# Two of six blocks of exponentials go through ScalarE and GpSimd instead of ScalarE and VectorE, in a kernel of attention and two expert layers

## The chip, the cores and the metric

The kernel runs on one core of one Trainium2 chip. The metric is device time in microseconds (us) from one launch; lower is better. The engines are TensorE (PE in the profile; its weight loads are listed apart as PEld), VectorE (DVE), ScalarE (ACT), GpSimd (POOL) and SyncE (SP), which issues the DMAs.

## The reference

Attention over 16 heads (2 batches of 8) of 768 positions and 64 dimensions, in which a query sees only the keys that fall to the same of 16 centroids, then two expert layers:

```python
mask = q_assign[:, :, :, None] == k_assign[:, :, None, :]
scores = scale * np.matmul(q, k.transpose(0, 1, 3, 2))
scores = np.where(mask, scores, -1000000000.0)
attn = np.exp(scores - np.max(scores, axis=-1, keepdims=True))
attn = attn / (np.sum(attn, axis=-1, keepdims=True) + 1e-09)
out = np.matmul(attn, v)
...
g = softplus(x @ w_in)            # 512 -> 2048
x = g @ w_out                     # 2048 -> 512
P = sinkhorn(exp(x @ w_gate))     # 8 rounds, 8 experts
out += P[:, e:e + 1] * (np.maximum(x @ w1[e], 0.0) @ w2[e])
```

## The kernel before

**Attention.** Two heads make a pair; there are eight pairs. The 768 queries of a head are cut in two, so that a pair is four halves, and the stage is a run of 32 halves, numbered `i`. For a half, `score` makes three tiles of scores (128 queries by 768 keys, four products each on TensorE, L478), VectorE takes each tile's maximum (L486), and ScalarE makes the exponentials `E` with their sum (L491).

`e_trans(i, s, ph)` then treats the keys in six blocks `s` of 128. Phase 0 turns a block of the half's three `E` tiles on TensorE into one PSUM tile `t` of 128 keys by 384 queries (L518, three transposes). The product with the values is to be more precise than one rounded product, so the block is split into a rounded part and a rest: phase 1 copies `t`, rounded, to `eh` in SBUF (ScalarE, L521), and phase 2 takes `el = t - eh` (VectorE, L525). `av(i, s)` adds the two products with the values, `eh` and `el`, to one PSUM tile `av` of the half (L533). `merge` takes that tile out (ScalarE L545, VectorE L547) and, at each second half, divides by the sums (VectorE L549).

**What a pair needs besides**, made ahead of time for a later pair: splitting queries and keys (`HL`; ScalarE L336, then GpSimd L344 and L345), splitting the values (`VV`; GpSimd L49 and L361), and finding each position's centroid (`sm`, `tp`, `po` on TensorE, copies by ScalarE, `A`, `mx` and `OH` on VectorE L402 to L410, with one product on GpSimd, L405, and one step, L413). `copy_r` at L49 is GpSimd's copy with rounding; `rw` spreads the sums, also there. Late in the stage GpSimd splits the four parts of the first layer's input (`chA`, `clA`; L49 and L99). Early in it the first weights, which come as 64-bit numbers, are converted to 32 bits by `to32` (L119 to L123, ScalarE and VectorE).

**What sets the order.** Every piece of work is put on a list with a time counted in steps; six steps are one half. The list is sorted by that time and traced in this order, and a scheduler then orders each engine's own queue by what is ready; the queues are fixed before the run, and each engine takes its queue in that order. A block's transposes stand at step `6 * i + s`, its products `AVL = 2` steps later.

**Buffers.** The PSUM tiles `t` (with `sm`, `tp`, `po`, `rb`) have three buffers, the score tiles two, `av` one; `eh` and `el` have four each, `E` seven.

The two expert layers follow (L631 and L684 the first products, L740 and L759 the second). Their code is not touched, and in the changed kernel each engine's queue holds the same instructions in the same order there.

Of the kernel before, what the change touches and what calls it, by code (L numbers as in the profile page):

```python
# [7 lines left out]
F32 = mybir.dt.float32  # L8
F32R = mybir.dt.float32r
# [3 lines left out]
ALU = mybir.AluOpType  # L13
# [7 lines left out]
def attention_moe_moe2(ctx, tc, v, qt, kt, centroids, w_in, w_out, w_gate, w1, w2, eye, out, dbg=None):  # L21
    nc = tc.nc
# [6 lines left out]
    P = 128  # L29
    NT = S // P  # L30
    HT = NT // 2
    CB = HT * P
# [15 lines left out]
    def copy_r(out_, in_):  # L48
        nc.gpsimd.tensor_scalar(out_, in_, 1.0, 0.0, ALU.mult, ALU.add)  # L49
# [193 lines left out]
    ap = slot_pool["ap"] = att.enter_context(tc.tile_pool(name="ap", bufs=2))  # L243
# [67 lines left out]
    def at(step, fn, cat=None):  # L311
        events.append((step, len(events), fn, cat))
# [147 lines left out]
            P_(g * SP - 21.67 + 2 * j, "v", pair_vsplit, j)  # L460

    EB = 7
    AH, FU = -5, -3
    Et, SC, RB, EHL, AVt, TT, TM, RW = {}, {}, {}, {}, {}, {}, {}, {}

    def half(i):
        g, r = divmod(i, 4)
        hf, j = divmod(r, 2)
        return pairs[g], j, hf

    def score(i, t, ph):
        st, j, hf = half(i)
        if ph == 0:
            c = (hf * HT + t) * P
            ps = Et[i, t] = ps_s.tile([P, 2, 512], F32, tag="s", name=f"s{i}_{t}")
            for m, X in enumerate((st.AT, st.Bt)):
                for kk in range(2):
                    nc.tensor.matmul(  # L478
                        ps[:, kk, 0:CB], X[0, j][:, c : c + P], X[1, j][:, kk * CB : (kk + 1) * CB],
                        start=m == 0, stop=m == 1,  # L480
                    )
            return
        if ph == 1:
            if t == 0:
                SC[i] = SC[i - 1] if j else ap.tile([P, 3, 2, HT], F32, tag="sc", name=f"sc{i}", bufs=3)
            nc.vector.tensor_reduce(SC[i][:, 0, j, t : t + 1], Et[i, t][:, :, 0:CB], AX.XY, ALU.max, negate=True)  # L486
            return
        sc = SC[i]
        if ph == 2:
            e = ap.tile([P, S], F32, tag="E", name=f"E{i}_{t}", bufs=EB)  # L490
            nc.scalar.activation(  # L491
                e.rearrange("p (a c) -> p a c", a=2), Et[i, t][:, :, 0:CB], AF.Exp,
                bias=sc[:, 0, j, t : t + 1], scale=1.0, accum_out=sc[:, 1, j, t : t + 1],
            )
            Et[i, t] = e
            return
        if ph == 3:

            nc.vector.tensor_scalar(sc[:, 2], sc[:, 1], 1e-9, None, ALU.add)
            nc.vector.reciprocal(sc[:, 2], sc[:, 2])  # L500
            return
        if ph == 4:
            rw = ap.tile([P, HT, P], F32, tag="rw", name=f"rw{i}", bufs=1)
            copy_r(
                rw.rearrange("p t (j d) -> p t j d", j=2),
                sc[:, 2].rearrange("p j t -> p t j").unsqueeze(3).to_broadcast([P, HT, 2, D]),
            )
            RW[i] = rw
            return
        rb = RB[i] = ps_t.tile([P, CB], F32, tag="t", name=f"rb{i}")  # L510
        for t_ in range(HT):
            nc.tensor.transpose(rb[:, t_ * P : (t_ + 1) * P], RW[i][:, t_, :], idf)

    def e_trans(i, s, ph):
        if ph == 0:
            pt = TT[i, s] = ps_t.tile([P, CB], F32, tag="t", name=f"t{i}_{s}")
            for t in range(HT):
                nc.tensor.transpose(pt[:, t * P : (t + 1) * P], Et[i, t][:, s * P : (s + 1) * P], idf)  # L518
        elif ph == 1:
            eh = ap.tile([P, CB], F32R, tag="eh", name=f"eh{i}_{s}", bufs=4)  # L520
            nc.scalar.copy(eh, TT[i, s])  # L521
            EHL[i, s] = eh
        else:
            el = ap.tile([P, CB], F32R, tag="el", name=f"el{i}_{s}", bufs=4)
            nc.vector.tensor_tensor(el, TT.pop((i, s)), EHL[i, s].bitcast(F32), ALU.subtract)  # L525
            EHL[i, s] = EHL[i, s], el

    def av(i, s):
        st, j, hf = half(i)
        if s == 0:  # L530
            AVt[i] = ps_a.tile([P, CB], F32, tag="a", name=f"av{i}")
        for n, m in enumerate(EHL.pop((i, s))):
            nc.tensor.matmul(  # L533
                AVt[i], st.VV[j][:, s, :], m, start=s == 0 and n == 0, stop=s == NT - 1 and n == 1
            )

    def merge(i, ph):
        st, j, hf = half(i)
        lo, hi = (slice(0, D), slice(D, P))
        main, other = (lo, hi) if j == 0 else (hi, lo)  # L540
        if j == 0 and ph == 0:
            TM[i] = TM[i + 1] = ap.tile([P, CB], F32, tag="tmp", name=f"tmp{i}", bufs=2)
        tmp = TM[i]
        if ph == 0:
            nc.scalar.copy(tmp[main], AVt[i][other])  # L545
        elif ph == 1:
            nc.vector.tensor_tensor(tmp[main], AVt.pop(i)[main], tmp[main], ALU.add)  # L547
        else:
            nc.vector.tensor_tensor(xt[st.b][:, st.hp, hf * CB : (hf + 1) * CB], tmp, RB.pop(i), ALU.mult)  # L549
# [6 lines left out]
    AVL = 2  # L556
# [3 lines left out]
    for i in range(NHALF):  # L560
        g = i // 4
        for t in range(HT):
            n = 6 * i + 2 * t - LEAD
            for ph, d in enumerate((0.28, 0.47, 2.31)):
                at(n + d, lambda i=i, t=t, ph=ph: score(i, t, ph), (f"s{ph}", g))
        if i % 2:
            at(n + 2.42, lambda i=i: score(i, 0, 3), ("s3", g))
            at(6 * i + 3.9, lambda i=i: score(i, 0, 4), ("rw", g))
            at(6 * i + 5 + AVL + 0.04, lambda i=i: score(i, 0, 5), ("rb", g))
        for s in range(NT):  # L570
            n = 6 * i + s
            for ph in range(3):
                at(n, lambda i=i, s=s, ph=ph: e_trans(i, s, ph), (f"e{ph}", g))
            at(n + AVL + 0.05, lambda i=i, s=s: av(i, s), ("av", g))
        for ph, d in enumerate((0.06, 1.22, 1.99)[: 2 + i % 2]):
            at(6 * i + 5 + AVL + d, lambda i=i, ph=ph: merge(i, ph), (f"m{ph}", g))
    at(14, lambda: fetch_first(0), ("fr", 0))
# [284 lines left out]
    for n, u in enumerate(units):  # L862
# [59 lines left out]
        if hold and held == NHOLD - 1:  # L922
            run(queue)
            for lu, q, cols in late:
                if (0, lu[2]) not in PB:
                    load_p(0, lu[2])
                g = GF[lu, q][:, cols]
# [41 lines left out]
```

## Time and profile before

| | |
|---|---|
| median of three runs | 1612.45 us (1611.81 to 1612.92) |
| the profiled execution | 1614.17 us, its span 1612.3 us |
| granted clock of TensorE, mean | 0.995 |
| PE busy over the span | 1539.4 us (95%) |
| PEld | 1383.9 us (86%) |
| DVE | 1060.6 us (66%) |
| ACT | 837.2 us (52%) |
| POOL | 640.2 us (40%) |

The shares are means over two different stages: attention up to 285.42 us, where the last `av` tile is taken out, and the expert layers after it. Over the whole span PE is busiest; that says little about the first stage, which is the one that the change touches. Matmuls are pipelined and their ends are modelled, so the time from one weight load to the next is the better measure of what TensorE needs.

### The profile page before, as it was taken

To read this page: it belongs to the slowest core of one execution; us is meant where nothing else is said; L and a number is where in the kernel's file an instruction comes from. 1 tells how busy PE (TensorE), PEld (TensorE's weight loads), DVE (VectorE), ACT (ScalarE), POOL (GpSimd) and SP (SyncE) were. 2 spreads that over 40 slices of the span, in tenths; PEclk is the share of its full clock that TensorE was granted. 3 is DMA by queue.
4 is the path that set the end of the run, shared out by engine and by line. 5 is a ranking of instruction groups with operands and counts; after the bars stand their busy time and mean duration, and the time that the engine had idled before them with its cause. 6 is when DMAs were issued, how large, how long until landed. Compare 5 with 4: busy or idle time off the path is not lost.

```text
span 1612.3 us, 22512 instructions
## 1 busy us (share of the span) xinstructions
PE 1539.4 (95%) x8110; PEld 1383.9 (86%) x8110; DVE 1060.6 (66%) x1723; ACT 837.2 (52%) x1685; POOL 640.2 (40%) x611
## 2 busy tenths in 40 slices
PE   5899999989999999999999999989999999999998
PEld 4788888878897878899999999978999999999997
DVE  4899999998454768665555655577555556556563
ACT  4888888766576754343443434344434434343342
POOL 2323322334655743433334433345333343333440
PEclk9999999999999999999999999999999999999999
DMA  8556420464211211322223222223223222222211
GB/s 222 156 152 153 128 65 6 141 219 133 77 53 53 65 53 55 84 59 82 82 60 88 64 77 79 72 66 115 67 75 89 57 85 71 71 88 63 79 53 47
DMA packets 132545, 141.24 MB, mean 88 GB/s; under 512 B 9072, under 2 KB 96592, under 8 KB 132432
## 3 DMA queue, kind: packets, MB, share of 16 engines
q1 hardware_dynamic: 132288, 139.72, 30.5%
q8 instruction: 64, 1.05, 0.3%
q14 instruction: 49, 0.40, 0.1%
q10 hardware_dynamic: 144, 0.07, 0.0%
HBM read 107.72 MB, written 11.58 MB: 74 GB/s over the span
## 4 chain that ended last, share of the span: by engine, by line
PE 65%; DVE 7%; ACT 4%; issue 1%; POOL 1%; DMA 1%; DVEq 0%; SPq 0%; ACTq 0%; POOLq 0%
PE Y L759 32%; PE la L631 16%; PE mb L631 8%; PE lb L631 4%; PE y L740 2%; DVE gf L707 1%; DVE gl L721 1%; DVE wl L226 1%; ACT gh L720 1%; ACT u L705 1%; PE p L684 1%; ACT u L704 1%; DMA r<-in_moe_w_out_dram 1%; DVE xS L75 0%; ACT u L706 0%
## 5 line engine op out<-in xcount | busy, mean ns | idle before, releaser
L720 ACT CAST gh<-gf 128x384 fp32r<-128x384 f32 x316 | 161.3, 513 | 479.0 <-DVE gf L714 434.5
L214 POOL TENSOR_TENSOR wf<-wf 128x256 f32<-128x256 f32 x288 | 235.0, 837 | 344.9 <-DMA wf<-in_moe_w_dram 289.6
L232 POOL TENSOR_TENSOR w2l<-w2f,w2h 128x512 fp32r<-128x512 f32 x160 | 236.3, 1496 | 323.2 <-ACT w2h L231 323.2
L759 PE MATMUL Y<-w2h,gh 128*128 128x512 f32 x768 | 299.3, 390 | 0.6 <-ACT gh L720 0.6
L759 PE MATMUL Y<-w2l,gh 128*128 128x512 f32 x768 | 299.2, 390 | 0.0
L759 PE MATMUL Y<-w2h,gl 128*128 128x512 f32 x768 | 298.8, 390 | 0.0
L721 DVE TENSOR_TENSOR gl<-gf,gh 128x384 fp32r<-128x384 f32 x316 | 201.1, 640 | 95.9 <-ACT gh L720 89.3
L658 DVE TENSOR_TENSOR gf<-la,c 128x384 f32<-128x384 f32 x71 | 39.5, 557 | 254.5 <-PE la L631 254.2
L225 ACT CAST wh<-wf 128x512 fp32r<-128x512 f32 (+1 forms) x232 | 153.0, 684 | 39.0 <-PE la L631 28.8
L759 PEld LDWEIGHTS Y<-w2h,gl 128*128 128x128 f32 x768 | 144.2, 188 | 29.8
L759 PEld LDWEIGHTS Y<-w2h,gh 128*128 128x128 f32 x768 | 144.1, 188 | 22.2 <-ACT gh L720 1.1
L759 PEld LDWEIGHTS Y<-w2l,gh 128*128 128x128 f32 x768 | 144.3, 188 | 21.0
L226 DVE TENSOR_TENSOR wl<-wf,wh 128x512 fp32r<-128x512 f32 (+1 forms) x194 | 151.4, 806 | 0.9 <-ACT wh L225 0.9
L714 DVE SCALAR_TENSOR_TENSOR gf<-gf,pb 128x384 f32<-128x384 f32 x177 | 149.3, 844 | 4.0
L525 DVE TENSOR_TENSOR el<-t,eh 128x384 fp32r<-128x384 f32 x192 | 102.4, 549 | 10.0 <-ACT eh L521 8.7
L486 DVE TENSOR_REDUCE sc<-s 128x1 f32<-128x768 f32 x96 | 91.1, 950 | 20.7 <-PE s L478 20.6
L521 ACT CAST eh<-t 128x384 fp32r<-128x384 f32 x192 | 91.4, 480 | 21.9 <-PE t L518 13.1
L518 PE MATMUL t<-idf,E 128*128 128x128 f32 x576 | 98.1, 278 | 4.8 <-ACT OHT L426 2.8
L631 PE MATMUL mb<-chS,wh 128*128 128x384 f32 x288 | 98.4, 342 | 4.3 <-DVE gf L654 4.0
L231 ACT CAST w2h<-w2f 128x512 fp32r<-128x512 f32 x160 | 92.2, 617 | 16.9 <-PE y L740 8.7
L631 PE MATMUL la<-chA,wh 128*128 128x384 f32 x288 | 98.0, 340 | 1.9 <-DVE gf L714 1.9
L631 PE MATMUL la<-chS,wh 128*128 128x384 f32 x288 | 97.9, 340 | 0.2 <-ACT c L650 0.2
(181 smaller groups left out, 3381.9 us busy)
## 6 DMA issues: line engine op xcount, KB each, us to landing
w2f<-in_moe_w_dram SPq DMA_DIRECT2D x128, 256.0 KB, 3.2
wf<-in_moe_w_dram SPq DMA_DIRECT2D x128, 256.0 KB, 3.3
AT<-HL SPq DMA_DIRECT2D x64, 192.0 KB, 4.0
r<-in_moe_w_in_dram SPq DMA_DIRECT2D x16, 512.0 KB, 5.7
r<-in_moe_w_out_dram SPq DMA_DIRECT2D x16, 512.0 KB, 4.9
Bt<-HL SPq DMA_DIRECT2D x32, 192.0 KB, 4.0
pb<-pdram SPq DMA_DIRECT2D x15, 384.0 KB, 7.3
w<-wf SPq DMA_DIRECT2D x16, 256.0 KB, 3.4
```

The source lines that it names most:

```text
L214: nc.gpsimd.tensor_tensor(wf[:, SLOT[o_], :], wf[:, SLOT[u_], :], wf[:, SLOT[v_], :], ALU.subtract)
L225: nc.scalar.copy(wh[:, c0:c1], wf[:, c0 + o : c1 + o, :])
L226: (nc.vector if kind == 2 or u == (1, 0, 0, 0) else nc.gpsimd).tensor_tensor(wl[:, c0:c1], wf[:, c0 + o : c1 + o, :], wh[:, c0:c1].bitcast ...
L231: nc.scalar.copy(w2h[:, c], w2f[c])
L232: nc.gpsimd.tensor_tensor(w2l[:, c], w2f[c], w2h[:, c].bitcast(F32), ALU.subtract)
L518: nc.tensor.transpose(pt[:, t * P : (t + 1) * P], Et[i, t][:, s * P : (s + 1) * P], idf)
L525: nc.vector.tensor_tensor(el, TT.pop((i, s)), EHL[i, s].bitcast(F32), ALU.subtract)
L631: nc.tensor.matmul(ps, wt[:, s_, ks], xx[:, k_, :], start=i in (0, 1, 3) and n == 0, stop=n == 3 * nk - 1, skip_group_check=True,)
L714: nc.vector.scalar_tensor_tensor(g, src, 0.0, PB[sb, e][:, cols], ALU.max, ALU.mult)
L720: nc.scalar.copy(gh[:, cols], g)
L721: nc.vector.tensor_tensor(gl[:, cols], g, gh[:, cols].bitcast(F32), ALU.subtract)
L759: nc.tensor.matmul(y[m], gt[:, ms], wt[:, q, :], start=first and i == 0, stop=last and i == 2)
```

## The change

Of the six blocks of a half, those with `s` 0 and 3 take another way. ScalarE copies the PSUM tile unrounded to a new SBUF tile `tf` (two buffers); GpSimd makes the rounded part `ph` from it (`copy_r`) and the rest `pl = tf - ph` (two buffers each). The products of these two blocks come at step `+ 2.03` instead of `+ 0.05`, that is about two steps later. As block 0 is then no longer the first to be multiplied, block 1 opens the sum in PSUM.

```diff
+    BY_POOL, AV_FIRST = (0, 3), 1
...
+        elif s in BY_POOL:
+            if ph == 1:
+                pt, tf = TT[i, s], ap.tile([P, CB], F32, tag="tf", name=f"tf{i}_{s}", bufs=2)
+                nc.scalar.copy(tf, pt)
+                TT[i, s] = tf
+                return
+            tf = TT.pop((i, s))
+            eh = ap.tile([P, CB], F32R, tag="ph", name=f"ph{i}_{s}", bufs=2)
+            el = ap.tile([P, CB], F32R, tag="pl", name=f"pl{i}_{s}", bufs=2)
+            copy_r(eh, tf)
+            nc.gpsimd.tensor_tensor(el, tf, eh.bitcast(F32), ALU.subtract)
+            EHL[i, s] = eh, el
...
-        if s == 0:
+        if s == AV_FIRST:
             AVt[i] = ps_a.tile([P, CB], F32, tag="a", name=f"av{i}")
...
-                AVt[i], st.VV[j][:, s, :], m, start=s == 0 and n == 0, stop=s == NT - 1 and n == 1
+                AVt[i], st.VV[j][:, s, :], m, start=s == AV_FIRST and n == 0, stop=s == NT - 1 and n == 1
...
-            at(n + AVL + 0.05, lambda i=i, s=s: av(i, s), ("av", g))
+            at(n + AVL + (2.03 if s in BY_POOL else 0.05), lambda i=i, s=s: av(i, s), ("av", g))
```

On TensorE, in half 16 (pair 4), the queue before held the products in the order of the blocks. These rows begin behind the transposes of block 4 (`t16_4`); `s18_0` is a score tile of half 18.

```order
L533 MATMUL av16_2230<-eh16_2_2226,VV40_1753 128x384
L533 MATMUL av16_2230<-el16_2_2228,VV40_1753 128x384
L478 MATMUL s18_0_2274<-AT410_1593,AT400_1547 128x384 x2
L478 MATMUL s18_0_2274<-Bt410_1594,Bt400_1548 128x384 x2
L518 MATMUL t16_5_2288<-idf_65,E16_0_2049 128x128
L518 MATMUL t16_5_2288<-idf_65,E16_1_2105 128x128
L518 MATMUL t16_5_2288<-idf_65,E16_2_2155 128x128
L533 MATMUL av16_2230<-eh16_3_2252,VV40_1753 128x384
L533 MATMUL av16_2230<-el16_3_2254,VV40_1753 128x384
```

The same place of the changed kernel, again behind the transposes of block 4; `ph16_0` and `pl16_0` are the parts of block 0 that GpSimd made.

```order
L546 MATMUL av16_2321<-ph16_0_2249,VV40_1800 128x384
L546 MATMUL av16_2321<-pl16_0_2250,VV40_1800 128x384
L546 MATMUL av16_2321<-eh16_2_2292,VV40_1800 128x384
L546 MATMUL av16_2321<-el16_2_2294,VV40_1800 128x384
L479 MATMUL s18_0_2342<-Bt410_1638,Bt400_1592 128x384
L519 MATMUL t16_5_2356<-idf_65,E16_0_2109 128x128
L519 MATMUL t16_5_2356<-idf_65,E16_1_2164 128x128
L519 MATMUL t16_5_2356<-idf_65,E16_2_2219 128x128
```

Block 0 is now multiplied after block 1 and just ahead of block 2, and block 3 (not in these rows) after block 4, ahead of block 5. From a block's transposes to its products TensorE now passes some three further blocks of transposes, one score tile and about two blocks' products.

On GpSimd, in the same half, the queue before held only what a later pair needs and the `rw` tiles.

```order
L49 TENSOR_SCALAR VV51_2281<-rawv5_1661 128x6x64
L361 TENSOR_TENSOR VV51_2281<-rawv5_1661,VV51_2281 128x6x64
L345 TENSOR_TENSOR HL16_2301<-rT16_2133,HL16_2301 128x768
L405 TENSOR_TENSOR A5_2038<-A5_2038,wsel_89 128x384
L413 TENSOR_SCALAR OH5_2299<-OH5_2299 128x6x32
```

The changed kernel has the new copies and differences between them.

```order
L49 TENSOR_SCALAR ph16_0_2249<-tf16_0_2247 128x384
L530 TENSOR_TENSOR pl16_0_2250<-tf16_0_2247,ph16_0_2249 128x384
L49 TENSOR_SCALAR VV51_2349<-rawv5_1707 128x6x64
L361 TENSOR_TENSOR VV51_2349<-rawv5_1707,VV51_2349 128x6x64
L405 TENSOR_TENSOR A5_2098<-A5_2098,wsel_89 128x384
L345 TENSOR_TENSOR HL16_2367<-rT16_2195,HL16_2367 128x768
L49 TENSOR_SCALAR ph16_3_2317<-tf16_3_2315 128x384
L530 TENSOR_TENSOR pl16_3_2318<-tf16_3_2315,ph16_3_2317 128x384
L49 TENSOR_SCALAR ph17_0_2375<-tf17_0_2373 128x384
L530 TENSOR_TENSOR pl17_0_2376<-tf17_0_2373,ph17_0_2375 128x384
L413 TENSOR_SCALAR OH5_2365<-OH5_2365 128x6x32
```

`ph16_3` now waits in the queue behind the two `VV` instructions, `A5` and `HL16` of the next pair, and `OH5` behind the parts of the next half's block 0. In halves 26 and 27 the four `chA` and four `clA` instructions stand in the same way between `ph` and `pl` instructions.

On VectorE, the conversion of the first weights is placed otherwise. In the changed kernel these rows stand between `x0` of half 3 and `el4_4`, the rest of block 4 of half 4 (`cm`, `wf0` and `w2f` are the conversion; `sc` the maxima of score tiles).

```order
L122 SCALAR_TENSOR_TENSOR wf0_590<-r10_584,wf0_590 128x512
L487 TENSOR_REDUCE sc6_898<-s6_2_959 128x1
L487 TENSOR_REDUCE sc6_898<-s7_0_1008 128x1
L123 SCALAR_TENSOR_TENSOR wf0_590<-r10_584,wf0_590 128x512
L120 TENSOR_SCALAR cm001_2180<-cm001_2180 128x512
L487 TENSOR_REDUCE sc6_898<-s7_1_1036 128x1
L121 TENSOR_SCALAR wf0_590<-cm001_2180 128x512
L487 TENSOR_REDUCE sc6_898<-s7_2_1070 128x1
L122 SCALAR_TENSOR_TENSOR wf0_590<-r10_584,wf0_590 128x512
L120 TENSOR_SCALAR cm010_2222<-cm010_2222 128x512
L123 SCALAR_TENSOR_TENSOR wf0_590<-r10_584,wf0_590 128x512
```

They are the core of a run of 21 instructions (six maxima, eleven of the conversion) without a block's rest between them. Before, the conversion was spread from half 4 to half 15, and behind `x0` of half 3 the rests of blocks 3 to 5 of half 4 came after five other instructions.

## Rows read from the trace of the kernel before

**Rows 1.** Busy time of each engine in the two stages, attention first.
```profile
core 0: us, PE busy (x) PEld busy (x) DVE busy (x) ACT busy (x) POOL busy (x), PEclk, DMA share, GB/s
0.00:285.42 285.42, 249.95 (x1554) 223.89 (x1554) 242.76 (x451) 222.08 (x489) 86.36 (x113) 0.99 0.47 125
285.42:1612.30 1326.88, 1289.46 (x6556) 1159.97 (x6556) 817.79 (x1272) 615.12 (x1197) 553.89 (x498) 1.00 0.27 80
```

**Rows 2.** Same view: four stretches of four halves each, 126.07 to 252.35; the next stretch.
```profile
sum 126.28, PE 118.41 PEld 107.63 DVE 118.38 ACT 107.86 POOL 43.06; mean PE 29.60 PEld 26.91 DVE 29.60 ACT 26.96 POOL 10.77
...
252.35:280.54 28.19, 26.37 (x173) 24.01 (x173) 25.70 (x47) 23.42 (x53) 4.62 (x4) 1.00 0.00 1
```

**Rows 3.** Groups of VectorE, 126.07 to 252.35: count, busy us, mean ns, idle before.
```profile
L525 DVE TENSOR_TENSOR el<-t,eh 128x384 fp32r<-128x384 f32 x97 | 51.9, 548 | 2.8 <-ACT eh L521 2.2
L486 DVE TENSOR_REDUCE sc<-s 128x1 f32<-128x768 f32 x48 | 45.6, 950 | 3.2 <-PE s L478 3.2
```

**Rows 4.** Waits of weight loads, 126.07 to 252.35: us, times, longest.
```profile
PEld av L533 <- DVE el L525: 3.2, 4, 0.9
PEld t L518 <- ACT OHT L426: 2.9, 4, 0.7
```

**Rows 5.** Timeline of weight loads in half 20: start us, us, instruction.
```profile
203.08 0.19 PEld L533 LDWEIGHTS av<-eh,VV 128*128 128x128 f32 x1
203.36 0.42 PEld L518 LDWEIGHTS t<-idf,E 128*128 128x128 f32 x3
203.76 0.19 PEld L533 LDWEIGHTS av<-eh,VV 128*128 128x128 f32 x1
...
204.75 0.36 PEld L478 LDWEIGHTS s<-AT,AT 128*128 128x128 f32 x2
205.44 0.42 PEld L518 LDWEIGHTS t<-idf,E 128*128 128x128 f32 x3
206.68 0.19 PEld L533 LDWEIGHTS av<-el,VV 128*128 128x128 f32 x1 [0.65 <-DVE el L525]
```

**Rows 6.** Groups of ScalarE, 126.07 to 252.35.
```profile
L521 ACT CAST eh<-t 128x384 fp32r<-128x384 f32 x96 | 45.9, 481 | 8.0 <-PE t L518 5.3 <-PE av L533 0.5
L376 ACT COPY sT<-sm 128x384 f32<-128x384 f32 x8 | 3.8, 471 | 0.0
```

**Rows 7.** Groups of GpSimd, 126.07 to 252.35.
```profile
L345 POOL TENSOR_TENSOR HL<-rT,HL 128x768 fp32r<-128x768 f32 x6 | 11.3, 1890 | 3.1 <-ACT HL L336 2.8
L361 POOL TENSOR_TENSOR VV<-rawv,VV 128x384 fp32r<-128x384 f32 x8 | 8.1, 1010 | 0.7
L49 POOL TENSOR_SCALAR VV<-rawv 128x384 fp32r<-128x384 f32 x8 | 4.1, 512 | 19.8 <-PE av L533 19.8
...
L405 POOL TENSOR_TENSOR A<-A,wsel 128x384 f32<-128x384 f32 x4 | 4.0, 1006 | 5.5 <-DVE sc L499 5.0 <-DVE A L403 0.5
L99 POOL TENSOR_TENSOR clA<-x,chA 128x768 fp32r<-128x768 f32 x2 | 3.6, 1844 | 0.0
L49 POOL TENSOR_SCALAR chA<-x 128x768 fp32r<-128x768 f32 x4 | 3.3, 837 | 0.0
```

**Rows 8.** Two VectorE lines: ns min/median/max, first and last start.
```profile
L525 DVE TENSOR_TENSOR el<-t,eh x192: 507/550/560, 34.2 to 284.3; 128x384 fp32r<-128x384 f32 x192
...
L403 DVE TENSOR_TENSOR A<-A,mx x8: 547/621/1033, 14.9 to 236.2; 128x384 f32<-128x384 f32 x8
```

**Rows 9.** Timeline around the longest L403, GpSimd and VectorE.
```profile
171.48 1.84 POOL L345 TENSOR_TENSOR HL<-rT,HL 128x768 fp32r<-128x768 f32 x1 [1.40 <-ACT HL L336]
...
172.70 1.03 DVE L403 TENSOR_TENSOR A<-A,mx 128x384 f32<-128x384 f32 x1
```

**Rows 10.** Busy time of each engine in halves 4 and 5 (columns of rows 1).
```profile
67.78:80.73 12.95, 9.84 (x59) 8.12 (x58) 12.65 (x25) 9.59 (x20) 6.58 (x8) 0.96 0.59 151
80.73:89.51 8.78, 8.12 (x43) 7.15 (x44) 6.71 (x14) 6.21 (x14) 1.13 (x1) 0.67 0.37 91
```

## The prediction

> **What bounds the kernel now.** I read the two stages first, since the change touches one alone. Attention takes 285.42 of 1612.30 us; the expert layers keep every queue as it was, so their 1326.88 us stay as a block and move with the end of attention [rows 1]. The whole effect has to come out of the 285 us, in which VectorE is busy for 242.76 and TensorE loads weights for 223.89.
>
> Next I cut the steady part of attention into stretches of four halves, one pair's worth. Four of them take 126.28 us, 31.57 each. In 31.57 us VectorE is busy for 29.60, ScalarE for 26.96, GpSimd for 10.77 [rows 2]. VectorE is idle for only 1.97 us of a stretch (6%). TensorE has to be measured by pitch. A block, three transposes and its two products, takes 203.08 to 203.76, 0.68 us; the transposes alone 203.36 to 203.76, 0.40, so 0.13 each and 0.28 for the products; a score tile 204.75 to 205.44, 0.69 [rows 5]. A stretch has 24 blocks (16.3), 12 score tiles (8.3), 8 products for the centroids at a quarter of a score tile (1.4) and 18 more transposes (2.4): 28.4 us. TensorE could thus do a stretch in 28.4 and takes 31.57, because VectorE is the slowest hand: the longest waits of its weight loads are for `el` (3.2 us in four stretches; in half 20 it stood 0.65 us for one) and for a copy behind a crowded ScalarE (2.9) [rows 4, 5]. In the last stretch, with nothing to prepare, VectorE's load falls to 25.70 and the time to 28.19 [rows 2]: the time follows VectorE's load.
>
> **The change part by part.**
>
> *Removed from VectorE:* 8 of 24 `el` in a stretch at 0.548 us, 4.4 us [rows 3]. VectorE falls from 29.60 to 25.2.
>
> *ScalarE:* each rounded copy becomes a plain one. The nearest rows are 0.481 us rounded and 0.471 unrounded, both out of PSUM [rows 6]; between -0.01 and 0 us each, taken as 0. ScalarE stays at 27.0. The PSUM tile of these blocks is free after one copy, no longer after copy and `el`.
>
> *Added to GpSimd:* per block a `copy_r` (0.512) and a difference (1.010), the same shape as the split of the values [rows 7]: 1.52 us, 12.2 for 8 blocks. GpSimd rises from 10.8 to 23.0 us of a stretch of about 30. It has the time, but not at every moment (below).
>
> *TensorE:* the same products, so 28.4 stays. After the change it needs most, then ScalarE 27.0, VectorE 25.2, GpSimd 23.0. For a stretch the bounds are 28.4 (no wait at all, -3.2) and 31.57 (another wait takes the place of `el`, 0). I take TensorE's need plus the idle time that the busiest engine had before: 28.4 + 1.97 = 30.4, a gain of 1.2. For halves 6 to 27, that is 5.5 stretches, -6.6 us (bounds 0 and -17.6).
>
> *Last four halves:* weight loads are 24.01 there against 26.91 [rows 2], so TensorE's need is about 28.4 - 2.9 = 25.5; with 1.97 idle 27.5 instead of 28.19: -0.7 (bounds 0 and -2.7).
>
> *The wait that is added:* TensorE waits for `pl`, behind ScalarE and GpSimd. From the end of a block's transposes to its products its queue holds some four blocks' transposes, five pairs of products and a score tile or more, about 4.1 us at full pace. The new way is 0.48 + 0.51 + 1.01 = 2.0 us. So 2 us are left, if GpSimd is free. Behind a late `pl` stand all of TensorE's queue, and on GpSimd `OH` and `rw`, for which `po` and `rb` wait. `tf` has two buffers: a GpSimd that is two blocks late stops ScalarE, and with it the exponentials.
>
> *Where GpSimd is tight:* in half 16 `VV`, `A5` and `HL16` stand ahead of `ph16_3`. From the last product of half 15, which frees the buffer for `VV`, GpSimd needs 0.51 + 1.01 + 1.01 + 1.89 + 0.51 + 1.01 = 5.9 us [rows 7]; TensorE's queue up to the products of block 3 holds 5.6 us at full pace and 6.0 at the pace of 30.4. That is just in time: I count 0, and 1.9 (one `HL`) as the upper bound each time.
>
> *The input splits in halves 26 and 27:* four `chA` at 0.84 and four `clA` at 1.84 [rows 7] stand among three `ph`/`pl` pairs: 3.3 + 7.4 + 4.6 = 15.3 us of GpSimd where TensorE passes in 3 x 3.8 = 11.4. Of the 3.9 us the 2 in hand go off: TensorE stands for about 2 us. +2 (0 to +4).
>
> *The conversion in half 4:* half 4 took 12.95 us, and VectorE was busy for 12.65 of it; in half 5 the granted clock was 0.67, a mix of the levels 1.2 and 2.4 GHz, after a half in which TensorE was busy for only 9.84 of 12.95 [rows 10]. The run of 21 instructions now does much the same: six maxima at 0.95 and fifteen at the 0.51 of that half (12.65 / 25) are 13.3 us, against some 6 us of TensorE's queue. So half 4 stays as bad as it was. But half 5 then finds its scores made and VectorE nearly free; it took 8.78, and without three score tiles needs 7.1 - 2.1 = 5.0. I take -2: the bounds are -3.8 and +2.9, which is a second stay of 5.8 us at the lower level (0.33 of 8.78 us is lost). Halves 0 to 3: 0.
>
> *Does GpSimd slow VectorE?* `el` took 507 to 560 ns over all 192 [rows 8], with GpSimd busy or not: nothing is added there. But L403, which reads SBUF twice, took between 0.547 and 1.033 us, and the longest began while an `HL` was running (171.48 to 173.32) and ended 0.41 after it [rows 8, 9]. One L403 a stretch is +0.5 at most, on a VectorE with 5 us to spare: 0. [...]
>
> *Sum:* -6.6 - 0.7 + 2 - 2 = -7.3. The profiled execution was 1614.17 us, 1.9 more than its span and 1.7 above the median of the runs, 1612.45. 1614.17 - 7.3 = 1606.9, less 1.7: **1605 us**.
>
> **The rivals.**
>
> *TensorE gets all it asks for.* Nothing but its own need is left: -17.6 - 2.7 - 2, about -22, 1590; I give this case what lies below 1599. For it: all three other engines have at least 1.4 us less to do per stretch. Against it: in no stretch now does the busiest engine run without idle time, and ScalarE's 27.0 is close behind. 0.12.
>
> *ScalarE takes VectorE's place, so that nothing is gained.* The change doesn't relieve it: 27.0 us are in its queue in a fixed order, it copies, exponentiates and splits, and every block passes through it. Now it is idle for 4.6 us of a stretch, mostly for `t` and the maxima; if the chain transposes, copy, exponential, scores has its own length near 31 us, `el` was only its visible end. Then the stretch stays within 0.6 of 31.57, and the time within 3.2 us of 1612.45. Against it: the waits for `el` come first, and `OHT` is late behind work that partly waits for VectorE itself [rows 4, 6]. 0.22.
>
> *GpSimd is late and the kernel gets slower.* Place: `pl` behind an `HL`, `VV` or `A` of the next pair. If TensorE waits for one `HL` (1.89) per stretch, the stretch is 30.4 + 1.9 = 32.3, +0.7; over 5.5 stretches +3.9, and with the -0.7 for the last halves, +4 for the input splits and -2, about +5: 1618. With two per stretch it is 34.2 and about +16: 1628. It decides from 1.2 us of waiting for `pl` per stretch on. For it: the margin in half 16 is nil, and `A` and `HL` wait for VectorE and ScalarE in their turn. Against it: the load is 23 of 30 us, and at most places 2 us are in hand. The Trainium skill speaks for it ("GPSIMD Engine Reference", "Engine selection"): elementwise work belongs on VectorE, since GpSimd takes about twice as long for two inputs. The trace agrees on the ratio (1.010 against 0.548); by that rule the 8 differences cost 3.7 us more than they save, which is a loss only where GpSimd is waited for. 0.16.
>
> **How the numbers follow.** Forecast (1599 to 1609.2) 0.50, full gain 0.12, no change (1609.2 to 1615.7) 0.22, slower 0.16. A measurement of this kernel tells about 0.2%, 3.2 us, from no change. Faster: 0.50 + 0.12 = 0.62; same 0.22; slower 0.16. The range 1596 to 1616 leaves out the larger part of the slower case (about 0.13) and half of the full gain (0.06).
>
> **What would show it.** Right: the expert layers' 1326.9 us unchanged; attention ending near 278; stretches near 30.4 with VectorE busy for some 25 to 26, GpSimd for 23, TensorE's weight loads for 26.9 as now; waits for `el` nearly gone; `tf` copies at 0.47 to 0.48; one wait for `pl` of about 2 us in halves 26 and 27. Wrong: waits of TensorE or ScalarE for `pl` in every pair (GpSimd late), stretches of 31.5 with ScalarE's waits for TensorE grown (no gain), `el` longer than 0.56 while GpSimd works (contention), or a longer stay at 1.2 GHz around half 4 or in the input splits.

## The result and the profile after

The changed kernel takes 1627.69 us (median of four runs, 1626.45 to 1628.77) against 1612.13 for the kernel before, run beside it: a ratio of 1.0086, 95% interval 1.0073 to 1.0099. It is slower by 0.9%, and outside the range that was given.

The two stages of the profiled execution (columns as in [rows 1]):

```profile
0.00:299.38 299.38, 255.78 (x1554) 224.20 (x1554) 221.47 (x387) 221.94 (x489) 184.33 (x241) 0.94 0.46 119
299.38:1627.00 1327.62, 1289.90 (x6556) 1159.77 (x6556) 821.11 (x1272) 615.06 (x1197) 554.49 (x498) 1.00 0.27 80
```

The expert layers stayed as they were (1327.62 against 1326.88). Attention ends 13.96 us later, although VectorE is busy for 21.3 us less in it. The start of each half's merge (the first ScalarE copy of its `av` tile) cuts the stage into pieces that can be laid beside each other. Up to half 3's merge, where half 4 is counted from, the new kernel is 1.46 us later; half 4 takes 22.02 instead of 12.95 (+9.07); half 5 8.11 instead of 8.78 (-0.67); halves 6 to 25 157.83 instead of 157.53 (+0.30); from there to the end of attention 42.18 instead of 38.38 (+3.80). That is all of the 13.96. In the last piece halves 26 and 27, where the input splits are, take 17.63 instead of 13.64 (+3.99), and the rest 0.19 less.

The steady stretches, four of them (halves 10 to 25) from merge to merge, answer to [rows 2], which is 126.28 us long:

```profile
131.28:257.20 125.92, 119.30 (x777) 106.94 (x777) 102.71 (x176) 107.19 (x238) 84.07 (x106) 1.00 0.41 99
```

VectorE is busy for 25.7 us of a stretch of 31.48, GpSimd for 21.0, ScalarE for 26.8: the loads are as forecast, the length is not. What TensorE's weight loads now wait for in it (beside [rows 4]):

```profile
PEld av L546 <- DVE tmp L560: 5.2, 11, 1.0
PEld po L420 <- POOL OH L413: 4.0, 4, 1.7
PEld t L519 <- ACT E L492: 1.8, 8, 0.4
...
PEld av L546 <- POOL pl L530: 0.6, 2, 0.3
PEld av L546 <- DVE el L538: 0.5, 1, 0.5
```

Two rows of the same view of the kernel before, halves 10 to 25:

```profile
PEld po L420 <- POOL OH L413: 2.7, 4, 0.7
PEld av L533 <- DVE tmp L547: 1.2, 3, 0.8
```

The wait for `el` has nearly gone, as it should, and that for `OHT` (ScalarE's copy of `po`) too; longer waits for the merge (`tmp`) and for `OH` stand in their place. With all rows of the view added up, TensorE's weight loads waited for 14.5 us in these four stretches before and wait for 15.6 now. `pl` is hardly waited for.

Halves 4 and 5 (beside [rows 10]), and TensorE's waits in half 4:

```profile
69.24:91.26 22.02, 13.73 (x60) 10.43 (x59) 19.24 (x31) 12.17 (x25) 10.98 (x11) 0.72 0.49 130
91.26:99.37 8.11, 7.61 (x45) 6.62 (x44) 5.68 (x10) 5.87 (x13) 4.92 (x7) 0.71 0.61 168
```

```profile
PEld t L519 <- ACT tf L523: 3.9, 2, 3.1
PEld s L479 <- ACT E L492: 3.6, 3, 1.9
PEld av L546 <- DVE el L538: 2.1, 1, 2.1
PEld av L546 <- POOL pl L530: 1.3, 1, 1.3
```

VectorE in half 4, the first instruction of the run of 21 and the `el` behind it, then the weight load that waits for this `el` (all between left out):

```profile
72.14 0.55 DVE L402 TENSOR_REDUCE mx<-A 128x24 f32<-128x384 f32 x1
87.13 1.01 DVE L538 TENSOR_TENSOR el<-t,eh 128x384 fp32r<-128x384 f32 x2
```

```profile
87.73 0.29 PEld L546 LDWEIGHTS av<-el,VV 128*128 128x128 f32 x1 [2.08 <-DVE el L538]
```

And GpSimd in halves 26 and 27, with the three weight loads that wait for it (all loads between them, and GpSimd's rows after the third `clA`, left out):

```profile
263.50 0.52 POOL L49 TENSOR_SCALAR ph<-tf 128x384 fp32r<-128x384 f32 x1
263.97 1.83 POOL L99 TENSOR_TENSOR clA<-x,chA 128x768 fp32r<-128x768 f32 x1
265.75 1.01 POOL L530 TENSOR_TENSOR pl<-tf,ph 128x384 fp32r<-128x384 f32 x1
266.71 1.84 POOL L99 TENSOR_TENSOR clA<-x,chA 128x768 fp32r<-128x768 f32 x1
268.51 0.83 POOL L49 TENSOR_SCALAR chA<-x 128x768 fp32r<-128x768 f32 x1
269.43 1.82 POOL L99 TENSOR_TENSOR clA<-x,chA 128x768 fp32r<-128x768 f32 x1
271.22 0.51 POOL L49 TENSOR_SCALAR ph<-tf 128x384 fp32r<-128x384 f32 x1
```

```profile
266.82 0.19 PEld L546 LDWEIGHTS av<-pl,VV 128*128 128x128 f32 x1 [1.63 <-POOL pl L530]
...
271.78 0.19 PEld L546 LDWEIGHTS av<-ph,VV 128*128 128x128 f32 x1 [1.67 <-POOL ph L49]
272.85 0.19 PEld L546 LDWEIGHTS av<-pl,VV 128*128 128x128 f32 x1 [0.89 <-POOL pl L530]
```

A `clA` of 1.83 us lies between a `ph` and its `pl`, and three instructions of 4.5 us ahead of the next `ph`.

### The profile page after: what moved, and what is told of

Read it like the earlier page. It is cut to its first block, busy times and chain, and to the rows that moved or that the text cites. A ratio compares the mean times of both kernels' runs of the same rounds, so it can differ in the third digit from the quotient of the medians.

```text
span 1627.0 us, 22559 instructions
## 1 busy us (share of the span) xinstructions
PE 1545.7 (95%) x8110; PEld 1384.0 (85%) x8110; DVE 1042.6 (64%) x1659; ACT 837.0 (51%) x1685; POOL 738.8 (45%) x739
## 3 DMA queue, kind: packets, MB, share of 16 engines
q1 hardware_dynamic: 132288, 139.72, 30.4%
## 4 chain that ended last, share of the span: by engine, by line
PE 65%; DVE 7%; ACT 4%; issue 1%; POOL 1%; DVEq 0%; ACTq 0%
PE Y L772 32%; PE la L644 16%; PE mb L644 9%; PE lb L644 4%; PE y L753 3%; DVE gf L720 1%; DVE gl L734 1%; PE p L697 1%; DVE wl L226 1%; ACT u L718 1%; ACT gh L733 1%; ACT u L717 1%; DVE xS L75 1%; ACT wh L225 1%; ACT u L719 1%
## 5 line engine op out<-in xcount | busy, mean ns | idle before, releaser
L727 DVE SCALAR_TENSOR_TENSOR gf<-gf,pb 128x384 f32<-128x384 f32 x177 | 154.8, 876 | 4.0
L644 PE MATMUL la<-clS,wh 128*128 128x384 f32 x288 | 97.7, 339 | 0.0
L644 PE MATMUL mb<-clS,wh 128*128 128x384 f32 x288 | 97.7, 339 | 0.0
```

The source lines that it names most:

```text
L644: nc.tensor.matmul(ps, wt[:, s_, ks], xx[:, k_, :], start=i in (0, 1, 3) and n == 0, stop=n == 3 * nk - 1, skip_group_check=True,)
L727: nc.vector.scalar_tensor_tensor(g, src, 0.0, PB[sb, e][:, cols], ALU.max, ALU.mult)
```

## The experiments

Theory A, formed from these two traces: the loss sits in two places, half 4 and the input splits; in the steady stretches other waits took the place of `el`. Rival B: GpSimd is late or in the way everywhere, and VectorE's relief by itself would have gained. The runs came in four sets, each beside runs of the kernel before on the same chip; its medians there were 1614.71 (e1 to e4), 1614.34 (e5 to e8), 1613.53 (e9 to e12) and 1613.73 (e13 to e15). Lengths of halves are from merge to merge.

### Where the loss sits

**e1**, the change from half 8 on:

```diff
-    BY_POOL, AV_FIRST = (0, 3), 1
+    def by_pool(i, s):
+        return s in (0, 3) and i >= 8
```

> Halves 0 to 7 are treated as before the change, halves 8 to 31 as after it. Theory A (the loss sits in two places, the run of conversions in half 4 and the input splits in halves 26 and 27, and the steady stretches are unchanged because other waits took the place of those for el): half 4 falls from 22 us back to about 13, the time from 1627.7 to about 1619. Theory B (GpSimd's added work costs a little everywhere, by late pl and by contention): a quarter of the halves is relieved, so a quarter of the 15 us goes, about 1624.

1619.74 us, 1.0037 (1.0025 to 1.0050). Half 4 is 12.95 us, the last halves stay long (half 27's interval 11.67).

**e2**, in halves 8 to 25 alone:

```diff
+        return s in (0, 3) and 8 <= i < 26
```

> Only halves 8 to 25 go through GpSimd, so both half 4 and halves 26 and 27 are as before the change. Theory A: both losses are gone and the steady stretches bring nothing, 1611 to 1615. Theory B: 18 of 32 halves still pay, about 1620. If the relief of VectorE gained in the steady stretches what the prediction said (1.2 us each), it would be 1607.

1616.52 us, 1.0007 (0.9994 to 1.0021): no difference that can be told, though the time itself lies above A's range. Both places are as before (half 4 12.96, half 27 7.07). Eighteen halves of the new way, with VectorE busy for 10 us less over attention (232.60), gain nothing. A has the places right; the little that it hoped to gain (down to 1611) isn't there.

**e3**, VectorE's relief without GpSimd's work. It leaves out the remainder of blocks 0 and 3 of the kernel before (the rounded part is multiplied twice):

```diff
+            if s in (0, 3):
+                TT.pop((i, s))
+                EHL[i, s] = EHL[i, s], EHL[i, s]
+                return
             el = ap.tile([P, CB], F32R, tag="el", name=f"el{i}_{s}", bufs=4)
```

> The kernel before, without the difference el in blocks 0 and 3 (the rounded part is multiplied twice in its place, so that part of the computation is left out): VectorE is relieved by the same 64 instructions, ScalarE keeps its copies, and GpSimd gets nothing. Theory A: stretches stay near 31.4 us, since TensorE then waits for the merge of the av tile and for po; half 4 is still long, about 20 us, because its queue on VectorE holds the same run of conversions; halves 26 and 27 are short; about 1620. Theory B: with nothing on GpSimd the relief shows as a gain, 1600 to 1606.

1622.39 us, 1.0058 (1.0046 to 1.0071): slower than before with strictly less work. Half 4 takes 20.67, four stretches 127.66:

```profile
127.11:254.77 127.66, 120.33 (x778) 106.65 (x777) 102.50 (x176) 106.59 (x239) 41.90 (x48) 1.00 0.39 97
```

VectorE is as free here as in the changed kernel and GpSimd as free as before [rows 2]. B falls: neither half 4 nor the missing gain is GpSimd's doing.

**e4**, the first product of a half one step later, so that it no longer waits for the merge of the half before:

```diff
-            at(n + AVL + (2.03 if s in BY_POOL else 0.05), lambda i=i, s=s: av(i, s), ("av", g))
+            at(n + AVL + (2.03 if s in BY_POOL else 1.01 if s == AV_FIRST else 0.05), lambda i=i, s=s: av(i, s), ("av", g))
```

> The changed kernel, with the first product of a half (block 1) put about one step later, behind the transposes of block 4, so that TensorE has one more block of transposes to do while the av tile of the half before is taken out. Theory A: the waits of the products for L560 (5.2 us in four stretches) go, 1.3 us a stretch, about 7 us: 1621, if no other wait takes their place in turn. Theory B: no change, 1627 to 1628.

1624.60 us, 1.0071 (1.0058 to 1.0084), between the two forecasts. The waits for `tmp` are gone from the list; waits for `tf` (2.7 us in three stretches), `pl` (2.7) and `el` (1.6) are there instead, and four stretches take 124.03: half a microsecond each. A wait that is listed isn't a time that can be had.

**e5**, the input splits off GpSimd (ScalarE rounds, VectorE subtracts):

```diff
-        if key == "1_0":
-            copy_r(hi, blk[name])
...
-        eng = nc.gpsimd if key == "1_0" or i in (1, 4, 5) else nc.vector
+        eng = nc.gpsimd if key != "1_0" and i in (1, 4, 5) else nc.vector
```

> The changed kernel with the four input splits near the end of attention taken off GpSimd: ScalarE rounds, VectorE subtracts. Theory A (the split queue on GpSimd holds up the new blocks there): the half of 11.57 us falls to 7.1 to 8, total 4 us below the changed kernel, about 1623.5. Theory B (GpSimd is late anyway, or VectorE and ScalarE pay as much for the splits): 1627 to 1629.

1624.91 us, 1.0060 (1.0044 to 1.0076). Half 27, which took 11.57, falls to 7.73, and from half 25's merge to the end of attention it takes 38.59 instead of 42.18 (before: 38.38). The +3.80 there is the split queue on GpSimd, as A says.

### What a steady stretch is long for

**e6** leaves out the second product in blocks 1 and 4, **e11** in blocks 1, 2, 4 and 5 of the changed kernel, **e7** in blocks 1 and 4 of the kernel before, each in halves 8 to 25; VectorE still makes the remainders.

```diff
-        for n, m in enumerate(EHL.pop((i, s))):
+        for n, m in enumerate(EHL.pop((i, s))[: 1 if s in (1, 4) and 8 <= i < 26 else 2]):
```

> The changed kernel with the second product (that of the remainder) left out in blocks 1 and 4 of halves 8 to 25; the remainder is still made by VectorE, so TensorE alone has less: 8 products of 0.175 us per stretch of four halves, 1.4 us. Theory A, sharpened by the first runs (TensorE itself is what a stretch takes 31.4 us for): stretches of 30.0 to 30.4, and 4.5 x 1.2 = 5 to 6 us less, 1621.5 to 1623. Theory C (a chain over ScalarE sets the length of a stretch, the second rival of the prediction): stretches of 31.2 to 31.6, 1627 to 1628.

> The kernel before with the same 36 products left out, its VectorE as busy as ever (29.6 us of 31.57 in a stretch). If VectorE bounded it, as the prediction said, or a chain over ScalarE (theory C): stretches of 31.3 to 31.6, 1611.5 to 1612.5. If TensorE did (theory A, sharpened): stretches near 30.3, 1606 to 1608.

> The changed kernel with the second product left out in all four blocks per half whose remainder VectorE makes (it still makes it), halves 8 to 25: TensorE has 16 products of 0.175 us, 2.8 us, less per stretch, where 8 fewer gave 0.8 of 1.4. If TensorE is what is left of the bound: stretches of 28.7 to 29.6, 1617 to 1620. If ScalarE's queue and what it waits for is (theory C): no further gain, stretches of 30.4 to 30.8, 1623 to 1625.

e6 1624.52 us, 1.0063 (1.0046 to 1.0080); e7 1613.09, 0.9995 (0.9984 to 1.0006); e11 1624.61, 1.0065 (1.0049 to 1.0081). Four stretches of each, in this order:

```profile
130.05:251.60 121.55, 113.01 (x745) 101.98 (x745) 101.13 (x176) 106.29 (x239) 84.38 (x105) 1.00 0.42 103
```

```profile
120.09:246.43 126.34, 114.60 (x746) 101.63 (x745) 119.33 (x217) 107.47 (x239) 41.82 (x47) 1.00 0.45 113
```

```profile
132.08:253.33 121.25, 109.80 (x714) 95.76 (x712) 101.26 (x176) 107.04 (x239) 84.45 (x105) 1.00 0.42 102
```

Beside the 126.30 of the same halves before and the 125.92 of the changed kernel: less for TensorE alone (e7) gains nothing; less for VectorE alone (e3) gains nothing; less for both (e6) gains 4.4 us on the changed kernel. Taking away twice as much from TensorE (e11) adds only 0.3. So, with the queues in the order they have here, either engine's load alone holds a stretch at 31.5 us or a little above, and something else holds it at about 30.3. The order counts beside the load: e4 has the loads of the changed kernel and takes 31.0. (e3's 31.9, above the 31.6 of before, has less work in it and another order; why it is the longer one stays open.) My sharpened theory, that TensorE itself is the 31.4 us, failed on e7; theory C, a chain over ScalarE of that length, failed on e6, whose ScalarE is as busy as ever. What the last limit is stays open; in e11 the longest sum of waits is that of `po` for `OH`, 7.3 us in four stretches (2.7 before).

### Half 4

**e8**, the conversions held at four places one pair apart:

```diff
-        at(92 + (n - 1) * 1.36, lambda n=n: fetch_first(n), ("fu", 0))
+        at(48 + (n - 1) * 24, lambda n=n: fetch_first(n), ("fu", 0))
...
-    KEEP = {'sp2': 1, 'fr': 0, 'av': 1, 'am3': 1, 'tpa': 1, 'smc': 0, 'm0': 1, 'rw': 1, 'pz': 1, 'e1': 1}
+    KEEP = {'sp2': 1, 'fr': 0, 'fu': 0, 'av': 1, 'am3': 1, 'tpa': 1, 'smc': 0, 'm0': 1, 'rw': 1, 'pz': 1, 'e1': 1}
```

> The changed kernel with the four conversions of the first weights, which its order gathers in half 4, held at four places, one pair apart, from half 8 on. Theory A (this run on VectorE is what half 4 takes 22 us for): half 4 near 8.2, each of the four halves that get a conversion 0 to 0.7 us longer, 12 us less in all: 1614 to 1617. Theory B (the new blocks themselves are late in the first halves, whatever VectorE does): half 4 stays above 12, 1620 or more.

A miss on both sides: 1631.53 us, 1.0106 (1.0089 to 1.0122). Half 4 still takes 19.15 without a single conversion in it, and the four stretches that got one (from half 8 on) are 2.0 to 3.4 us longer than in the changed kernel (34.85, 35.21, 34.11, 33.28). The gathered conversion is not, by itself, what half 4 is long for. Its trace shows six score tiles on TensorE with only one block's transposes among them, four of them waiting for an exponential. Hence theory D, and **e9** and **e10**, which hold the score tiles of halves 6 and 7 at their places, in the changed kernel and in the one before:

```diff
-                at(n + d, lambda i=i, t=t, ph=ph: score(i, t, ph), (f"s{ph}", g))
+                at(n + d, lambda i=i, t=t, ph=ph: score(i, t, ph), (f"s{ph}" + ("k" if i in (6, 7) else ""), g))
...
-    KEEP = {'sp2': 1, 'fr': 0, 'av': 1, 'am3': 1, 'tpa': 1, 'smc': 0, 'm0': 1, 'rw': 1, 'pz': 1, 'e1': 1}
+    KEEP = {'sp2': 1, 'fr': 0, 's0k': 0, 'av': 1, 'am3': 1, 'tpa': 1, 'smc': 0, 'm0': 1, 'rw': 1, 'pz': 1, 'e1': 1}
```

> The changed kernel with the score tiles of halves 6 and 7 held at their written places, so that TensorE no longer has six of them in a row in half 4; the conversions stay gathered in half 4. Theory D (formed after the spread conversions left half 4 at 19.15 us: six score tiles in a row, each waiting for an exponential, are what half 4 is long for): half 4 at 11 to 14, 8 to 10 us less in all, 1618 to 1621. Theory A as first put (the run of conversions does it): half 4 stays at 19 or more, 1625 or more.

> The kernel before with the same score tiles held at their places (there only three stand in a row). Theory D: half 4 falls from 12.95 to between 9 and 12, 1 to 4 us less in all, 1609 to 1612. If the conversions set its half 4, nothing changes: 1612 to 1614.

Misses again: e9 1625.36 us, 1.0069 (1.0055 to 1.0084), half 4 20.44; e10 1619.96, 1.0034 (1.0018 to 1.0049), half 4 12.70 and half 5 12.34. D falls as well. But side by side, e8 and e9 show what they share. TensorE's longest wait, e8 then e9, in half 4:

```profile
PEld s L479 <- ACT E L492: 3.7, 4, 1.4
```

```profile
PEld t L519 <- ACT tf L523: 8.8, 1, 8.8
```

And ScalarE's queue ahead of the `tf` of block 3, e8 then e9:

```profile
77.59 0.90 ACT L492 ACTIVATE E<-s,sc 128x768 f32<-128x768 f32 x1 [1.00 <-DVE sc L487]
78.39 0.19 ACT L492 ACTIVATION_READ_ACCUMULATOR E<-s,sc 128x1 f32 x1
78.48 1.56 ACT L336 ACTIVATE HL<-rT 128x768 fp32r<-128x768 f32 x2
79.95 0.46 ACT L523 COPY tf<-t 128x384 f32<-128x384 f32 x1
```

```profile
76.38 0.71 ACT L119 ACTIVATE cm<-r 128x512 f32<-128x512 f32 x1 [1.12 <-DVE wf L121]
78.51 0.67 ACT L119 ACTIVATE cm<-r 128x512 f32<-128x512 f32 x1 [1.43 <-DVE w2f L121]
79.08 1.57 ACT L336 ACTIVATE HL<-rT 128x768 fp32r<-128x768 f32 x2
80.55 0.46 ACT L523 COPY tf<-t 128x384 f32<-128x384 f32 x1
```

In both, the copy that TensorE needs stands behind things that wait for VectorE, exponentials in the one, absolute values of the conversion in the other, and then behind two `HL`. In the order of ScalarE's queue this can be read without any run. Before, from the copy of block 2 of half 4 to that of block 3:

```
L521 CAST eh4_2_818<-t4_2_814 128x384
L491 ACTIVATE E5_2_871,sc4_625<-s5_2_826,sc4_625 128x768
L336 ACTIVATE HL03_838<-rT03_737 128x768
L521 CAST eh4_3_844<-t4_3_840 128x384
```

The changed kernel:

```
L534 CAST eh4_2_836<-t4_2_832 128x384
L492 ACTIVATE E5_1_846,sc4_637<-s5_1_807,sc4_637 128x768
L492 ACTIVATE E5_2_891,sc4_637<-s5_2_841,sc4_637 128x768
L492 ACTIVATE E6_0_930,sc6_898<-s6_0_886,sc6_898 128x768
L492 ACTIVATE E6_1_964,sc6_898<-s6_1_925,sc6_898 128x768
L119 ACTIVATE cm001_2180<-r10_584 128x512
L492 ACTIVATE E6_2_1013,sc6_898<-s6_2_959,sc6_898 128x768
L492 ACTIVATE E7_0_1041,sc6_898<-s7_0_1008,sc6_898 128x768
L119 ACTIVATE cm010_2222<-r20_585 128x512
L336 ACTIVATE HL13_911<-rT13_753 128x768
L336 ACTIVATE HL03_853<-rT03_751 128x768
L523 COPY tf4_3_859<-t4_3_855 128x384
```

Two instructions stood there, now ten. In e3's trace nine stand there, and its half 4 takes 20.67. The copies of blocks are held at their written place from the second pair on, while exponentials, conversion and `HL` may move up. Theory E: this order is the cause, whichever instructions make it up. **e13** changes one number in the changed kernel, so that the copies of the second pair may move too; **e14** does it to the kernel before.

```diff
-    KEEP = {'sp2': 1, 'fr': 0, 'av': 1, 'am3': 1, 'tpa': 1, 'smc': 0, 'm0': 1, 'rw': 1, 'pz': 1, 'e1': 1}
+    KEEP = {'sp2': 1, 'fr': 0, 'av': 1, 'am3': 1, 'tpa': 1, 'smc': 0, 'm0': 1, 'rw': 1, 'pz': 1, 'e1': 2}
```

> The changed kernel with one number different: ScalarE's copies of the transposed blocks are held at their written place from the third pair on, no longer from the second, so that in halves 4 to 7 exponentials, absolute values of a conversion and splits of the next pair can't all be put ahead of the copy of block 3 of half 4. All of the change stays. Theory E (what half 4 is long for is the order of ScalarE's queue ahead of this copy; either the six exponentials or the conversions do it, as the two runs showed that took away only one): half 4 at 8 to 11, halves 5 to 8 together at most 2 longer, 1613 to 1618. If the new blocks are late there on their own account (theory B): half 4 above 14, 1620 or more.

> The kernel before with the same number. Its half 4 took 12.95, of which TensorE was busy for 9.84. Theory E: half 4 at 8 to 10, halves 5 to 8 up to 2 longer, 1608 to 1611. If VectorE, not the order, sets half 4 here: 1612 to 1615.

e13 1618.23 us, 1.0033 (1.0020 to 1.0046). Half 4, then halves 5 to 9:

```profile
67.50:74.23 6.73, 6.73 (x46) 6.25 (x45) 6.38 (x14) 5.82 (x13) 5.27 (x8) 1.00 0.83 176
74.23:122.67 48.44, 40.08 (x252) 35.36 (x251) 44.45 (x70) 37.56 (x83) 33.23 (x37) 0.96 0.56 151
```

The time is just above E's range. With all of the change in place half 4 falls from 22.02 to 6.73, below the forecast of E, and the granted clock stays at 1.00 in it. Halves 5 to 9, which now hold the conversions and some more matmuls (252 instead of 235), take 48.44 instead of 40.02, more than E allowed. Of the 15.3 us that half 4 gains 8.4 are lost again there; halves 4 to 9 take 55.17 instead of 62.04 (before: 52.96). E holds for half 4; the work that leaves it costs time where it goes. As this one number changes the order on every engine, VectorE's run of 21 is gone too: e13 shows that the held copies are the cause, not which queue behind them would have been enough. e14 is a miss: 1621.18 us, 1.0046 (1.0029 to 1.0062). Half 4 falls to 8.05, but half 5 takes 12.00, and halves 16 and 17, at and behind the last conversions, 10.90 and 11.93.

**e12** (e5's, e4's and e9's edits together) and **e15** (e5's, e4's and e13's):

> The changed kernel with the score tiles of halves 6 and 7 held at their places, the input splits off GpSimd and the first product of a half one step later. If the three losses are separate (theories A and D) they add up: 9 + 3.5 + 2.5 us less, 1612 to 1615, level with the kernel before and no better. If GpSimd's lateness is one loss that moves about (theory B), less than half of it comes back: 1620 or more.

> The changed kernel with that number, with the input splits off GpSimd and with the first product of a half one step later. Theory E: the losses are separate and add up, 1627.7 - 12 - 3.5 - 2 = 1609 to 1612, a little below the kernel before. Theory B: 1617 or more.

e12 1620.50 us, 1.0043 (1.0028 to 1.0058), a miss, and by its time alone in B's range: half 4 is still 20.05, since e9's edit doesn't mend it, and halves 26 and 27 are short (14.84). e15 1613.65 us, 0.9997 (0.9988 to 1.0006), attention ending at 284.75 (before: 285.42): above E's range and well below B's. By the traces the losses are separate and nearly add up: from the first merge to the last e13, e5 and e4 are 6.3, 3.1 and 2.7 us shorter than the changed kernel, 12.1 together, and e15 13.7. The medians, each beside the kernel before, are less clean (11.1, 5.0 and 5.7 us saved one by one, 15.6 by e15). Without these losses the change is worth nothing that can be measured, and no version here is told apart as faster than the kernel before.

## Why the prediction was wrong, point by point

**The loads** were right: VectorE 25.7 of a stretch against 25.2, ScalarE 26.8 against 27.0, GpSimd 21.0 against 23.0, the expert layers unchanged, waits for `el` nearly gone.

**-6.6 for 5.5 stretches: the step that failed first.** "TensorE's need plus the idle time that the busiest engine had before" took VectorE, busy for 94% of a stretch, for the one limit, and left TensorE no more than 2 us of waiting. Halves 6 to 25 changed by +0.30. The need of 28.4 is borne out: less the waits of its weight loads a stretch is 28.0 us before and 27.6 after. The wait is what failed. In four stretches those for `el` fell from 4.4 us to 1.0 and those for `OHT` from 2.9 to none, but those for `tmp` rose from 1.2 to 5.2 and those for `OH` from 2.7 to 4.0, so that TensorE waits for 3.9 us of a stretch where it waited for 3.6. This is the bound of no gain that the prediction itself named, another wait in the place of `el`. e3 shows that VectorE's relief is worth nothing by itself, e7 and e6 that TensorE's work counts only where VectorE is relieved too. The argument that the time follows VectorE's load, from the last stretch, didn't hold, because there TensorE has less to do too (weight loads 24.01 against 26.91) [rows 2]. The Trainium skill ("Perfetto Trace Analysis", "Identifying the Most-Contended Engine") has the rule that I followed: the engine with the highest occupancy is the one to be improved first. The trace doesn't bear it out here: by busy share that was VectorE (94%; TensorE's weight loads 85%), and 4 us less a stretch (e3: 25.6 instead of 29.6) gained nothing. Of the rivals, "no gain" came true for the stretches, but not for its reason: e6 went to 30.4 us with ScalarE's load unchanged.

**-2 for halves 4 and 5: the step that cost most.** It came out at +8.40. The prediction set the run of 21 instructions on VectorE, 13.3 us, equal to the whole half. In the trace the run takes 15.0 us (72.14 to 87.13), 2.9 us of the half lie ahead of it, and 4.1 behind it, in which TensorE still has the half's last products (of blocks 3 to 5) to do: 22.02 together. And it read VectorE's queue alone. On ScalarE ten instructions stand ahead of the one copy, of block 3, that TensorE needs (it frees the PSUM tile for the next transposes); where the conversions are gone from VectorE (e8) half 4 still takes 19.15, and where this copy may move (e13) 6.73. The bounds, -3.8 from half 5 and +2.9 from the clock, had no room for a longer half 4. In the lower clock the prediction named the right danger and made it too small: TensorE is busy for 13.73 us with 60 matmuls where it was for 9.84 with 59 [rows 10], so the lower clock can account for up to 3.9 of the 9.07; no run took it away alone.

**+2 for the input splits.** The mechanism was right and its size too small: 4.2 us of waits for `ph` and `pl`, and halves 26 and 27 3.99 us longer, at the upper bound of +4; e5 takes it away again. The last four halves gained 0.19 us of the 0.7. What the working added up as one queue has a `clA` between a `ph` and its own `pl`, and TensorE stands for each part in turn.

**0 for halves 0 to 3** measured +1.46; across the kernels of this study the first merge alone starts anywhere from 41.4 to 44.3 us, so this is not told apart from no change.

**GpSimd is late**, the rival on the slower side, gave 1618 and 1628 for one or two waits for an `HL` in each stretch. The time came out like this by luck, the mechanism didn't: `pl` is waited for 0.6 us in four stretches, and e3 loses its half 4 without any of GpSimd's new work.

## What to carry to other kernels

When each engine runs a queue of its own in a fixed order, a high busy share names a candidate, not the limit: a run that only leaves out the work in question (e3 here, four lines) tells before anything is built whether its time is to be had. A change that frees an engine also changes what a scheduler puts ahead; before pricing a stretch, read on every engine what now stands ahead of the first instruction that is held in place, and count what each of these waits for. Filler work isn't free because its engine has idle time: four conversions of 2.2 us, held at four places of their own (e8), made each stretch 2.0 to 3.4 us longer, though VectorE had 5.8 us idle in it.

## What the hardware showed beside

**VectorE and GpSimd.** In the prediction it was an instruction with two SBUF inputs (L403) that stood for GpSimd. In e9 one with a single input took far longer beside GpSimd, too:

```profile
80.16 2.04 DVE L121 TENSOR_SCALAR w2f<-cm 128x512 int32<-128x512 int32 x1
```

```profile
79.99 1.92 POOL L345 TENSOR_TENSOR HL<-rT,HL 128x768 fp32r<-128x768 f32 x1 [6.18 <-ACT HL L336]
```

It takes 0.42 us elsewhere (median 0.420 of 16 in the changed kernel), and ends 0.29 after the `HL`. An L123, two inputs, took 2.30 instead of 0.68 in half 4 of the changed kernel beside an `HL` of 2.05. Over attention L410 took 0.762 us on average instead of 0.551, and the sums' small step (L500, L499 before; six numbers a partition) 0.333 instead of 0.202; on a VectorE with 5.8 us idle per stretch e2 shows no price for it. The Trainium skill ("SBUF — State Buffer", "Who interferes with whom") names `tensor_scalar` among the operations that can enter a mode in which VectorE takes the port pair that it shares with GpSimd. The row agrees with that; no run shows which mode it was in.

**The clock.** In half 4 of the changed kernel (two microseconds a row):

```profile
74.00:76.00 2.00, 0.50 (x3) 0.50 (x4) 1.97 (x5) 1.54 (x3) 0.55 (x1) 1.00 0.82 254
76.00:78.00 2.00, 1.39 (x7) 0.81 (x5) 1.91 (x3) 1.43 (x4) 0.00 (x0) 1.00 0.03 10
78.00:80.00 2.00, 1.46 (x5) 1.33 (x6) 1.38 (x4) 1.48 (x4) 0.00 (x0) 0.73 0.07 26
80.00:82.00 2.00, 1.19 (x4) 0.68 (x3) 2.00 (x3) 0.73 (x2) 0.00 (x0) 0.50 0.28 106
```

TensorE was busy for 0.50, 1.39 and 1.46 us of the first three rows, while its score tiles waited for exponentials; in the third the granted clock fell from 1.00 towards 0.50, the level of 1.2 GHz, and it stayed there until about 96 us. So these waits are paid twice: in the wait, and at half the clock in the work behind it, the copy of block 3 and all that waits for it included.
